# A top-k attention and MLP kernel: dividing the exponentials on GpSimd before their split, instead of the outputs after it

## The chip, the cores and the metric

The kernel runs on one core of a Trainium2 chip. The metric is the time of one execution in device microseconds (us), as the median of several runs. The engines are named as in the profile: PE is TensorE (matmuls; PEld its weight loads), DVE is VectorE, ACT is ScalarE, POOL is GpSimd, and SP is the engine whose queue issues nearly all DMAs. Each engine works through its instructions strictly in the order in which the program gives them; semaphores tie the engines to one another.

## The reference

Two stages follow each other. The first is attention in which each query keeps its 32 largest scores:

```python
B, H, S, D = 8, 8, 576, 64
scores = (1 / np.sqrt(D)) * np.matmul(q, k.transpose(0, 1, 3, 2))
kth = np.partition(scores, -32, axis=-1)[..., -32:-31]
scores = np.where(scores >= kth, scores, -1000000000.0)
scores = scores - np.max(scores, axis=-1, keepdims=True)
attn = np.exp(scores)
attn = attn / (np.sum(attn, axis=-1, keepdims=True) + 1e-09)
attn_out = np.matmul(attn, v)
```

The second takes the 4608 tokens (batch times sequence, 512 wide) through `h = x @ w_in` (512 x 2048), `g = h / (1 + exp(-1.702 h))` and `g @ w_out` (2048 x 512). All data is float32.

## The kernel before, in words

**Slots.** The attention is cut into 144 slots, 18 for each of the 8 batches. A slot is 128 query rows of two heads (or, for the last 64 rows of the sequence, 64 rows of four heads). A slot's scores are two blocks of 128 x 576. It goes through these steps:

- `scores` (L282): PE multiplies q and k into two PSUM tiles (`s_ps`; the pool has two buffers, so one slot's scores fill it). `copy_scores` (L294): ACT brings them to SBUF as `sc` (four buffers).
- `topk_of_pairs`: DVE finds the 32nd largest score of every row, a slot at a time. The two halves of a row are compared element by element (`pair_up`, L323: the larger ones go to `greater`; POOL makes the smaller ones, `lesser`, in two integer instructions, L326 and L327). Then come rounds of "the eight largest" (L344) and "take them out" (L347) over the larger ones, `pair_up` for the next slot, and two rounds over the smaller ones; a merge (L351) and a minimum (L356) give `cut`. These are 23 calls, counted from 0; `pair_up` of the next slot is call 14, the two last L344 are calls 19 and 20.
- `lows` (L377): POOL works out the bias `low` of the exponentials.
- `exponentials`: ACT masks the scores in place (L397, two instructions) and takes the exponentials (L400, two instructions, whose sums over the rows go to `sums`).
- `split` (L470): ACT copies the exponentials, taken as 16-bit words, into two planes of upper and lower halves, which are written over `sc`; SP writes them to DRAM (`rows`, L472). `turn_by_dma` (L478): a transposing DMA reads them back as `pt`, keys on the partitions.
- `values_at` (L538): PE multiplies v and `pt` into `o`.
- Division: the exponentials are not divided. `invert` (L429, L431) has DVE invert the sums of two slots at once, POOL spreads each over 64 columns (`wide`, L433), and PE transposes them (`sum_rows`, L527) into the same PSUM tile as `o`. ACT copies the tile to SBUF (L954, 128 x 512) and POOL multiplies `o` by the inverses into `xT` (`x_of`, L552).

**The MLP beside it.** When all 512 columns of 128 tokens stand in `xT`, they are a block. `hidden` (L595) multiplies four tiles' worth with `w_in` on PE, `tanh` (L617, L620) takes the tanh and a copy on ACT, `gate` (L629, L630) joins them on POOL, and `project` (L650) multiplies with `w_out`; a finished block leaves through ACT (L658) and SP.

**The order.** It is written out by hand. Slots 0 to 12 are handled singly by `slot`, while the weights are loaded, by a form of the steps that turns the exponentials on PE; there `divide` (L408, L410, L413) makes diagonal matrices of the inverses. From slot 13 on, `two_slots(n)` handles two slots in each call, n = 13, 15, ... I call one call an iteration. It takes the first of its slots through mask, exponentials and split, searches slot n, gives PE one `hidden` and one `project`, multiplies the values of slots n-3 and n-2, makes the scores of slots n+2 and n+3, takes slot n through mask, exponentials and split, gives PE another `hidden` and `project`, and searches slot n+1. Since every engine keeps the program's order, the order of these calls is the order on ACT, DVE, POOL and SP.

**q and k.** The q and k of a later batch are made ready one pair of heads at a time: `prepare_by_dma` copies their halves apart on ACT (L240, 24 times), and SP writes and transposes them (L244 to L249, L253). Batch 1 is turned on PE and copied by ACT instead (`prepare`, L217 to L224). All these calls fall on odd slots, into `prepare_some(first)` of an iteration.

In every search the inversion is one call among the 23:

```python
if i == (13 if m < SETTLED + 4 else 8) and m % 2:
    invert(m - 2)
```

Of the kernel before, what the change touches and what calls it, by code (L numbers as in the profile page):

```python
# [30 lines left out]
def kernel(  # L31
# [286 lines left out]
    def pair_up(n):  # L318

        sc = st[n]["sc"]  # L320
        a, b = sc[:, :, 0:HALF], sc[:, :, HALF:S]
        greater[n] = lefts.tile([P, 2, HALF], F32, name="greater", tag="left")
        nc.vector.tensor_tensor(out=greater[n][:], in0=a, in1=b, op=ALU.max)  # L323
        lesser[n] = raws.tile([P, 2, HALF], F32, name="lesser", tag="raw")
        whole = lesser[n][:].bitcast(I32)
        nc.gpsimd.tensor_tensor(out=whole, in0=a.bitcast(I32), in1=greater[n][:].bitcast(I32), op=ALU.subtract)  # L326
        nc.gpsimd.tensor_tensor(out=whole, in0=whole, in1=b.bitcast(I32), op=ALU.add)  # L327

    def topk_of_pairs(n):

# [59 lines left out]

    def exponentials(n, between=lambda: None):

        sc, cut, low = st[n]["sc"], st[n]["cut"], st[n]["low"]
        pr = st[n]["pr"] = prp.tile([P, 2 * S], F32, name="pr")
        den = st[n]["den"] = sums_of(n) if n >= SETTLED else small.tile([P, 2], F32, name="den")[:]
        for i in range(2):
            nc.scalar.activation(sc[:, i, :], sc[:, i, :], AF.Prelu, bias=cut[:, i : i + 1], alpha=HUGE)  # L397
        between()
        for i in range(2):
            nc.scalar.activation(  # L400
                pr[:, i * S : (i + 1) * S], sc[:, i, :], AF.Exp, bias=low[:, i : i + 1],
                accum_out=den[:, i : i + 1],
            )

    def divide(n):

        some = small.tile([P, 2], F32, name="some", tag="sums")
        nc.vector.tensor_scalar_add(some[:], st[n]["den"], 1e-9)  # L408
        rden = small.tile([P, 2], F32, name="rden", tag="inverse")
        nc.vector.reciprocal(rden[:], some[:])  # L410
        by = st[n]["by"] = xs[:, 4, 0:2, :]
        for i in range(2):
            nc.gpsimd.tensor_scalar(by[:, i, :], ident[:], rden[:, i : i + 1], 1.0, op0=ALU.mult, op1=ALU.mult)  # L413

    sums = {}

    def sums_of(n):

        k = n // 2
        if k not in sums:  # L420
            sums[k] = small.tile([P, 2, 2], F32, name="sums")
        return sums[k][:, n % 2, :]

    def invert(n):

        k = n // 2
        if k in sums:
            total = sums[k][:]
            nc.vector.tensor_scalar_add(total, total, 1e-9)  # L429
            inverse = small.tile([P, 4], F32, name="inverse")  # L430
            nc.vector.reciprocal(inverse[:], total.rearrange("p s j -> p (s j)"))  # L431
            wide = sums[k] = raws.tile([P, 2, 2, D], F32, name="wide", tag="raw")
            nc.gpsimd.tensor_copy(  # L433
                out=wide[:].rearrange("p s j d -> p (s j) d"),
                in_=inverse[:].unsqueeze(2).to_broadcast([P, 4, D]),
            )

    def turn(n, first, blocks):
# [41 lines left out]
    places = {}  # L480
    free = [4, 0, 1, 2, 3]

    def x_at(b, t, hp):

        name = (b, t) if t < NF else b // 2
        if name not in places:
            at = free.pop(1 if name in ((0, 0), (0, 1), (0, 2), (0, 3)) else 0)
            places[name] = at
        x = xs[:, places[name], hp, :]
        return x if t < NF else x[:, b % 2 * TAIL : (b % 2 + 1) * TAIL]  # L490

    def values(n, put_off=None):
# [29 lines left out]
            put_off.append(bring)  # L522


    def sum_rows(m, to):

        nc.tensor.transpose(to, sums[m // 2][:, m % 2, :, :], ident[:])  # L527

    def values_at(m, o):

        b, t, hps = slots[m]
# [12 lines left out]
                    )  # L544
        st[m].clear()

    def x_of(m, o, by):

        b, t, hps = slots[m]
        for p in range(2 if t == NF else 1):  # L550
            cols = slice(p * TAIL, (p + 1) * TAIL) if t == NF else slice(0, P)
            nc.gpsimd.tensor_tensor(out=x_at(b, t, hps[p]), in0=o[:, cols], in1=by[:, cols], op=ALU.mult)  # L552
        finish_x(m)

    def finish_x(m):

# [115 lines left out]
    def leave_all():  # L672
        while leaving:
            leaving.pop(0)()
# [40 lines left out]
    def finish_one():  # L715
        unfinished.pop(0)()
# [74 lines left out]
    def slot(n):  # L791
# [7 lines left out]
        if n == 0:  # L799
            for piece in some:  # L800
                piece["low"]()
                piece["sign"]()
        else:
            bounds(n - 1)
            if n == PAIRED:
                pair_up(n)

            exponentials(n - 1, bring_all if n % 4 == 1 else lambda: None)
            copy_scores(n + 1)
            bring_all()  # L810
            while signs:
                signs.pop(0)()
            if 1 < n <= TURNS:
                turn_main(n - 2)
                turn_ends(n - 2)
            for piece in some:
                piece["size"]()
            tanh(False)
        for i, op in enumerate(topk_of_pairs(n) if n >= PAIRED else topk(n)):
            op()  # L820
            if i == 2 and n < SETTLED:
                for _ in range(min(3 if n >= TURNS else 6, len(unfinished))):
                    finish_one()
            if i == 5:
                if n > 0:
                    divide(n - 1)
                while unfinished:
                    finish_one()
            if i == 10:
                gate(False)  # L830
# [47 lines left out]
    def two_slots(n):  # L878

        first, second = [later.pop(m, []) for m in (n, n + 1)]  # L880
        live = lambda m: 0 <= m < N
        aside = n < N

        def begin(todo):
            for fn, args in todo:
                if fn is not prepare and fn is not prepare_by_dma:
                    fn(*args)

        def prepare_some(todo):
            for fn, args in todo:  # L890
                if fn is prepare or fn is prepare_by_dma:
                    fn(*args)

        def find(m):
            for i, op in enumerate(topk_of_pairs(m) if live(m) else [lambda: None] * 23):
                op()
                if i == (13 if m < SETTLED + 4 else 8) and m % 2:
                    invert(m - 2)
                if i > 1 and unfinished:
                    finish_one()  # L900

        def project_one():
            if may_project(0):
                project(True)

        def measure(m):
            if live(m):
                bounds(m)
            gate(aside)

        opens = n == SETTLED + 1
        ahead = n < SETTLED + 4
        begin(first)
        measure(n - 1)
        if ahead:
            scores(n + 2)
        if opens:
            bring_all()
        if live(n - 1):
            exponentials(n - 1)  # L920
            split(n - 1)
        if ahead:
            copy_scores(n + 2)
        if opens:
            leave_all()
            tanh(aside)
        find(n)
        hidden(ps_t if opens else None)
        project_one()
        tanh(aside)  # L930
        prepare_some(first)
        held = [m for m in (n - 3, n - 2) if live(m) and "rows" in st[m]]
        o = ps_t.tile([P, 2, 2, P], F32, name="o", tag="tp") if held else None
        for i, m in enumerate(held):
            sum_rows(m, o[:, i, 0, :])
        if live(n + 2) and not ahead:
            scores(n + 2)
            copy_scores(n + 2)
        leave_all()
        for i, m in enumerate(held):  # L940
            values_at(m, o[:, i, 1, :])
        if live(n - 1):
            turn_by_dma(n - 1)
        while turns:
            turns.pop(0)()
        if live(n + 3):
            scores(n + 3)
        begin(second)
        measure(n)
        def bring():  # L950
            if not held:
                return
            x = raws.tile([P, 2, 2, P], F32, name="x", tag="raw")
            nc.scalar.copy(out=x[:], in_=o[:])  # L954
            for i, m in enumerate(held):
                x_of(m, x[:, i, 1, :], x[:, i, 0, :])

        if live(n):
            exponentials(n, bring)
        else:  # L960
            bring()
        if live(n):
            split(n)
            turn_by_dma(n)
        hidden(ps_t)
        if live(n + 3):
            copy_scores(n + 3)
        tanh(aside)
        prepare_some(second)
        project_one()  # L970
        leave_all()
        find(n + 1)

    with tc.manual_schedule():
        opening()
# [36 lines left out]
```

## Time and profile before

| what | us |
|---|---|
| median of three runs (1468.69 to 1471.01) | 1469.49 |
| the profiled execution's own time | 1468.81 |
| its span in the trace | 1467.0 |
| busy: PE / DVE / ACT / POOL | 1430.7 / 1336.3 / 1173.9 / 863.1 |
| L527 on PE, busy, 132 instructions | 25.3 |
| L552 and L433 on POOL, busy | 60.1 and 27.2 |
| L470 on ACT, 132 instructions, mean of one | 2.112 |

Busy times of an engine count overlapping instructions once. Matmuls are pipelined: a record of one lasts longer than the step from its start to the start of the next, so steps are read from starts. In rows of groups the columns are the line, the engine, the operation, what it writes and reads, and its count, then busy us and the mean ns of one, then the idle time before. In rows of the timeline they are the start and the length in us, the engine, the line and the operation. In rows of waits they are who waited for whom, us in total, how often, and the longest.

### The profile page before, as it was taken

How to read it: one execution, taken by the hardware profiler on the slowest of the kernel's cores; microseconds unless marked ns; L12 is line 12 of the kernel's file. 1: busy time of each engine (PE TensorE's matmuls, PEld its weight loads, DVE VectorE, ACT ScalarE, POOL GpSimd, SP SyncE). 2: the span in 40 equal slices, each digit the busy share in tenths (PEclk: the TensorE clock that was granted, in tenths of full speed). 3: DMA queues.
4: the chain of work that ended last, by engine and by line, in shares of the span. 5: the costliest groups of instructions: out<-in, count | busy, mean ns of one | idle time of the engine just before them, and what ended most of it. 6: DMA issues, size and time to landing. Idle time of an engine off the chain costs nothing.

```text
span 1467.0 us, 29219 instructions
## 1 busy us (share of the span) xinstructions
PE 1430.7 (98%) x9696; PEld 1015.8 (69%) x9696; DVE 1336.3 (91%) x4541; ACT 1173.9 (80%) x1865; POOL 863.1 (59%) x1119
## 2 busy tenths in 40 slices
PE   7789989999999999999999999999999999999998
PEld 5667757777666667777666667777666667777665
DVE  7999999999999999999999999999999999999910
ACT  6998788978788887878888787888878787887730
POOL 3777655666566665666665666656665666655510
PEclk8899999999999999999999999999999999999999
DMA  7452356867677677676777676766766777544420
GB/s 218 142 159 73 86 155 187 209 173 193 175 177 190 171 179 200 179 188 176 170 176 200 181 189 177 195 179 171 178 186 185 189 171 187 153 135 124 131 78 15
DMA packets 516311, 242.04 MB, mean 165 GB/s; under 512 B 452672, under 2 KB 490560, under 8 KB 516160
## 3 DMA queue, kind: packets, MB, share of 16 engines
q1 hardware_dynamic: 515728, 239.89, 62.2%
q8 instruction: 76, 1.25, 0.4%
q14 instruction: 75, 0.61, 0.1%
q10 hardware_dynamic: 432, 0.30, 0.1%
HBM read 45.09 MB, written 102.24 MB: 100 GB/s over the span
## 4 chain that ended last, share of the span: by engine, by line
PE 82%; DVE 13%; ACT 2%; issue 1%; DMA 1%; SPq 1%; POOL 0%; POOLq 0%; DVEq 0%; ACTq 0%
PE ph L595 31%; PE po L650 30%; PE o L538 10%; PE s_ps L282 10%; DVE top L304 4%; DVE left L307 3%; DVE top L344 2%; DVE left L347 1%; PE o L527 1%; DMA rows<-sc 1%; DVE greater L323 0%; DMA pt<-rows 0%; DVE lesser L347 0%; DVE th L632 0%; ACT pr L400 0%
## 5 line engine op out<-in xcount | busy, mean ns | idle before, releaser
L595 PEld LDWEIGHTS ph<-xT,win 128*128 128x128 f32 x3520 | 484.1, 191 | 86.9 <-issue 57.4
L595 PE MATMUL ph<-xT,win 128*128 128x128 f32 (+1 forms) x3520 | 537.6, 309 | 1.4 <-POOL xT L552 1.2
L650 PE MATMUL po<-wout,th 128*128 128x512 f32 x1152 | 518.4, 593 | 1.1 <-ACT ob L658 1.1
L650 PEld LDWEIGHTS po<-wout,th 128*128 128x128 f32 x1152 | 213.2, 190 | 214.5 <-issue 207.1
L344 DVE MAX8 top<-left 128x8 f32<-128x288 f32 x792 | 325.4, 445 | 0.0
L470 ACT COPY sc<-pr 128x2304 uint16<-128x2304 uint16 x132 | 278.8, 2112 | 4.2
L294 ACT ACTIVATE sc<-s_ps 128x576 f32<-128x576 f32 x288 | 171.0, 646 | 136.2 <-PE s_ps L282 133.9
L347 DVE MATCH_REPLACE8 left<-top,left 128x288 f32<-128x288 f32 x528 | 229.7, 442 | 0.0
L326 POOL TENSOR_TENSOR lesser<-sc,greater 128x576 int32<-128x576 int32 x132 | 186.6, 1413 | 72.8 <-DVE greater L323 72.8
L552 POOL TENSOR_TENSOR xT<-x 128x128 f32<-128x128 f32 (+1 forms) x148 | 60.1, 429 | 285.6 <-ACT x L954 285.6
L400 ACT ACTIVATE pr<-sc,low 128x576 f32<-128x576 f32 x288 | 221.3, 777 | 0.0
L397 ACT ACTIVATE sc<-sc,cut 128x576 f32<-128x576 f32 x288 | 208.1, 779 | 8.5 <-POOL cut L388 5.9
L344 DVE MAX8 top<-lesser 128x8 f32<-128x288 f32 x528 | 213.8, 445 | 0.0
L327 POOL TENSOR_TENSOR lesser<-lesser,sc 128x576 int32<-128x576 int32 x132 | 186.5, 1413 | 10.4
L282 PE MATMUL s_ps<-qk_t 64*128 64x288 f32 (+1 forms) x1280 | 182.2, 431 | 0.2 <-ACT qk_t L218 0.2
L630 POOL TENSOR_TENSOR th<-th,h 128x512 f32<-128x512 f32 x128 | 163.3, 1275 | 10.7
L629 POOL TENSOR_SCALAR th<-th 128x512 f32<-128x512 f32 x128 | 79.4, 620 | 110.3 <-ACT th L617 110.1
L538 PE MATMUL o<-pt,v_l 128*64 128x128 f32 (+1 forms) x2368 | 143.5, 264 | 0.1
L323 DVE TENSOR_TENSOR greater<-sc 128x576 f32<-128x576 f32 x132 | 101.8, 771 | 41.0 <-ACT sc L294 40.4
L538 PEld LDWEIGHTS o<-pt,v_l 128*64 128x64 f32 x2368 | 119.7, 137 | 25.5 <-issue 23.5
L282 PEld LDWEIGHTS s_ps<-qk_t 64*128 64x128 f32 (+1 forms) x1280 | 99.1, 177 | 41.1 <-issue 22.3
L617 ACT ACTIVATE th<-ph 128x512 f32<-128x512 f32 x144 | 85.9, 597 | 43.8 <-PE ph L595 40.8
(83 smaller groups left out, 1462.8 us busy)
## 6 DMA issues: line engine op xcount, KB each, us to landing
rows<-sc SPq DMA_DIRECT2D x132, 576.0 KB, 3.1
qk_rows<-halves SPq DMA_DIRECT2D x48, 256.0 KB, 2.8
qk_l<-in_q_dram SPq DMA_DIRECT2D x64, 128.0 KB, 3.0
raw<-in_moe_w_in_dram SPq DMA_DIRECT2D x16, 512.0 KB, 4.7
v_l<-in_v_dram SPq DMA_DIRECT2D x32, 256.0 KB, 3.3
raw<-in_moe_w_out_dram SPq DMA_DIRECT2D x16, 512.0 KB, 3.6
out_dram<-ob SPq DMA_DIRECT2D x32, 256.0 KB, 2.9
qk_l<-in_k_dram SPq DMA_DIRECT2D x62, 128.0 KB, 2.8
```

The source lines that it names most:

```text
L282: nc.tensor.matmul(ps[i][rows, c, 0:HALF], lhsT=qT[b, hps[p]][on, cols], rhs=kT[b, hps[p]][on, FIRST[i] + c * HALF : FIRST[i] + (c + 1) * ...
L294: nc.scalar.mul(out=to, in_=ps[i][:, :, 0:HALF], mul=SCALE)
L326: nc.gpsimd.tensor_tensor(out=whole, in0=a.bitcast(I32), in1=greater[n][:].bitcast(I32), op=ALU.subtract)
L327: nc.gpsimd.tensor_tensor(out=whole, in0=whole, in1=b.bitcast(I32), op=ALU.add)
L344: nc.vector.max(found(r, i, True), src[:, i, :])
L347: nc.vector.match_replace(to[:, i, :], found(r, i), src[:, i, :], LOWEST)
L397: nc.scalar.activation(sc[:, i, :], sc[:, i, :], AF.Prelu, bias=cut[:, i : i + 1], alpha=HUGE)
L400: nc.scalar.activation(pr[:, i * S : (i + 1) * S], sc[:, i, :], AF.Exp, bias=low[:, i : i + 1], accum_out=den[:, i : i + 1],)
L470: nc.scalar.copy(out=halves, in_=pr[:].bitcast(U16).rearrange("p (k h) -> p h k", h=2))
L538: nc.tensor.matmul(o[j * D : (j + 1) * D, cols], lhsT=main[:, j, c, :] if c < NF else tail[:, j, :], rhs=pt[:, MAIN[j] + c if c < NF else ...
L595: nc.tensor.matmul(ph[:, i * many * P : (i + 1) * many * P], lhsT=win[:, c, f * P : (f + 1) * P], rhs=xs[:, first : first + step * (many - ...
L650: nc.tensor.matmul(x.po[:], lhsT=gT[:, i * P : (i + 1) * P], rhs=wout[:, f, :], start=(x.done == 0), stop=(x.done == FC - 1))
```

## The change

The exponentials of the slots from 12 on are divided by their sums before they are split. Per slot, DVE inverts the two sums (`invert`, now for one slot, two columns), and POOL multiplies the two blocks of 128 x 576 exponentials in place (`normalize`). `sum_rows`, the spreading over 64 columns and the multiplication behind the values go away; ACT copies `o` straight into `xT`, 256 columns for two slots.

The order changes with it. The inversion of slot n-1 stands in the search of slot n, behind call 20 for odd n and behind call 18 for even n. The split of slot n-1 moves from before the search of slot n to behind it, behind `normalize`; likewise for slot n and the search of n+1. The mask of an iteration's second slot moves ahead of the scores' copy, except where q and k are prepared in the iteration. POOL's second instruction of `pair_up` (L327) is put off behind `normalize` and `lows`. `hidden` and `project` of the first half stand ahead of the search in the program.

```diff
@@ pair_up @@
-        nc.gpsimd.tensor_tensor(out=whole, in0=whole, in1=b.bitcast(I32), op=ALU.add)
+        unpaired.append(n)
+    def pair_rest():
+        while unpaired:
+            n = unpaired.pop()
+            whole, b = lesser[n][:].bitcast(I32), st[n]["sc"][:, :, HALF:S]
+            nc.gpsimd.tensor_tensor(out=whole, in0=whole, in1=b.bitcast(I32), op=ALU.add)
...
+    def invert(n):
+        some = small.tile([P, 2], F32, name="some", tag="sums")
+        nc.vector.tensor_scalar_add(some[:], st[n]["den"][:], 1e-9)
+        rden = st[n]["rden"] = small.tile([P, 2], F32, name="rden", tag="inverse")
+        nc.vector.reciprocal(rden[:], some[:])
...
+    def normalize(n):
+        pr = st[n]["pr"][:].rearrange("p (i k) -> p i k", i=2)
+        for i in range(2):
+            nc.gpsimd.tensor_scalar(
+                pr[:, i, :], pr[:, i, :], st[n]["rden"][:, i : i + 1], 1.0, op0=ALU.mult, op1=ALU.mult
             )
...
-    def sum_rows(m, to):
-        nc.tensor.transpose(to, sums[m // 2][:, m % 2, :, :], ident[:])
...
+    def x_of(held, o):
+        b, t, hps = slots[held[0]]
+        x = xs[:, place_of(b, t), :, :]
+        if t < NF:
+            nc.scalar.copy(out=x[:, hps[0] : hps[0] + 2, :], in_=o[:])
+        else:
+            parts = o[:].rearrange("p s (h r) -> p (s h) r", h=2)
+            nc.scalar.copy(out=x[:, :, b % 2 * TAIL : (b % 2 + 1) * TAIL], in_=parts)
+        for m in held:
+            finish_x(m)
```

`two_slots` after the change, from the definition of `find` on (`opens` holds in the first call, `ahead` in the first two; `mask` and `exps` are the two halves of `exponentials`):

```python
def find(m):
    for i, op in enumerate(topk_of_pairs(m) if live(m) else [lambda: None] * 23):
        op()
        if i == (20 if m % 2 else 18) and live(m - 1):
            invert(m - 1)
...
def measure(m):
    if live(m):
        lows(m)
    pair_rest()
    gate(aside)
...
if live(n - 1):
    exponentials(n - 1)
...
hidden(ps_t if opens else None)
project_one()
find(n)
if live(n - 1):
    normalize(n - 1)
tanh(aside)
measure(n)
if live(n - 1):
    split(n - 1)
prepare_some(first)
late = any(fn is prepare or fn is prepare_by_dma for fn, args in first)
if live(n) and not late:
    mask(n)
held = [m for m in (n - 3, n - 2) if live(m) and "rows" in st[m]]
if live(n + 2) and not ahead:
    scores(n + 2)
    copy_scores(n + 2)
o = ps_t.tile([P, 2, P], F32, name="o", tag="tp") if held else None
for i, m in enumerate(held):
    values_at(m, o[:, i, :])
if live(n - 1):
    turn_by_dma(n - 1)
...
if live(n + 3):
    scores(n + 3)
begin(second)
if live(n) and late:
    mask(n)
if live(n):
    exps(n)
if held:
    x_of(held, o)
leave_all()
hidden(ps_t)
if live(n + 3):
    copy_scores(n + 3)
find(n + 1)
if live(n):
    normalize(n)
    split(n)
    turn_by_dma(n)
tanh(aside)
measure(n + 1)
prepare_some(second)
project_one()
leave_all()
```

More of the change, by code (lines that the diff above doesn't have):

```diff
@@ L326, in pair_up @@
         nc.gpsimd.tensor_tensor(out=whole, in0=a.bitcast(I32), in1=greater[n][:].bitcast(I32), op=ALU.subtract)
-        nc.gpsimd.tensor_tensor(out=whole, in0=whole, in1=b.bitcast(I32), op=ALU.add)
+        unpaired.append(n)
+    unpaired = []
+    def pair_rest():
[3 more added lines that the diff above has]
+            nc.gpsimd.tensor_tensor(out=whole, in0=whole, in1=b.bitcast(I32), op=ALU.add)
     def topk_of_pairs(n):
@@ L391, in exponentials, with mask, exps @@
     def exponentials(n, between=lambda: None):
-        sc, cut, low = st[n]["sc"], st[n]["cut"], st[n]["low"]
-        pr = st[n]["pr"] = prp.tile([P, 2 * S], F32, name="pr")
-        den = st[n]["den"] = sums_of(n) if n >= SETTLED else small.tile([P, 2], F32, name="den")[:]
+        mask(n)
+        between()
+        exps(n)
+    def mask(n):
+        sc, cut = st[n]["sc"], st[n]["cut"]
         for i in range(2):
             nc.scalar.activation(sc[:, i, :], sc[:, i, :], AF.Prelu, bias=cut[:, i : i + 1], alpha=HUGE)
-        between()
+    def exps(n):
+        sc, low = st[n]["sc"], st[n]["low"]
+        pr = st[n]["pr"] = prp.tile([P, 2 * S], F32, name="pr")
+        den = st[n]["den"] = small.tile([P, 2], F32, name="den")
         for i in range(2):
@@ L403, in exponentials @@
             )
+    def invert(n):
[3 more added lines that the diff above has]
+        nc.vector.reciprocal(rden[:], some[:])
     def divide(n):
[L407 to L410, printed above, removed]
+        invert(n)
         by = st[n]["by"] = xs[:, 4, 0:2, :]
         for i in range(2):
[L413 to L435, printed above, removed]
+            nc.gpsimd.tensor_scalar(by[:, i, :], ident[:], st[n]["rden"][:, i : i + 1], 1.0, op0=ALU.mult, op1=ALU.mult)
+    def normalize(n):
[3 more added lines that the diff above has]
+                pr[:, i, :], pr[:, i, :], st[n]["rden"][:, i : i + 1], 1.0, op0=ALU.mult, op1=ALU.mult
             )
@@ L481, with place_of, x_at @@
     free = [4, 0, 1, 2, 3]
-    def x_at(b, t, hp):
+    def place_of(b, t):
         name = (b, t) if t < NF else b // 2
         if name not in places:
-            at = free.pop(1 if name in ((0, 0), (0, 1), (0, 2), (0, 3)) else 0)
-            places[name] = at
-        x = xs[:, places[name], hp, :]
+            places[name] = free.pop(1 if name in ((0, 0), (0, 1), (0, 2), (0, 3)) else 0)
+        return places[name]
+    def x_at(b, t, hp):
+        x = xs[:, place_of(b, t), hp, :]
         return x if t < NF else x[:, b % 2 * TAIL : (b % 2 + 1) * TAIL]
@@ L545, in values_at @@
         st[m].clear()
[L547 to L553, printed above, removed]
+    def x_of(held, o):
[8 more added lines that the diff above has]
+            finish_x(m)
     def finish_x(m):
@@ L818, in slot @@
             tanh(False)
+        pair_rest()
         for i, op in enumerate(topk_of_pairs(n) if n >= PAIRED else topk(n)):
             op()
+            pair_rest()
             if i == 2 and n < SETTLED:
@@ L892, in prepare_some @@
                     fn(*args)
+        opens = n == SETTLED + 1
+        ahead = n < SETTLED + 4
         def find(m):
@@ L896, in find, with measure @@
                 op()
-                if i == (13 if m < SETTLED + 4 else 8) and m % 2:
-                    invert(m - 2)
+                if i == (20 if m % 2 else 18) and live(m - 1):
+                    invert(m - 1)
                 if i > 1 and unfinished:
                     finish_one()
+        def measure(m):
+            if live(m):
+                lows(m)
+            pair_rest()
+            gate(aside)
         def project_one():
@@ L904, in project_one @@
                 project(True)
-        def measure(m):
-            if live(m):
-                bounds(m)
+        begin(first)
+        if opens:
+            bounds(n - 1)
             gate(aside)
[L911 to L914, printed above, removed]
         if ahead:
@@ L920, in two_slots @@
             exponentials(n - 1)
-            split(n - 1)
         if ahead:
@@ L926, in two_slots @@
             tanh(aside)
-        find(n)
         hidden(ps_t if opens else None)
         project_one()
+        find(n)
+        if live(n - 1):
+            normalize(n - 1)
         tanh(aside)
+        measure(n)
+        if live(n - 1):
+            split(n - 1)
         prepare_some(first)
+        late = any(fn is prepare or fn is prepare_by_dma for fn, args in first)
+        if live(n) and not late:
+            mask(n)
         held = [m for m in (n - 3, n - 2) if live(m) and "rows" in st[m]]
-        o = ps_t.tile([P, 2, 2, P], F32, name="o", tag="tp") if held else None
-        for i, m in enumerate(held):
-            sum_rows(m, o[:, i, 0, :])
         if live(n + 2) and not ahead:
@@ L938, in two_slots @@
             copy_scores(n + 2)
-        leave_all()
+        o = ps_t.tile([P, 2, P], F32, name="o", tag="tp") if held else None
         for i, m in enumerate(held):
-            values_at(m, o[:, i, 1, :])
+            values_at(m, o[:, i, :])
         if live(n - 1):
@@ L948, in two_slots @@
         begin(second)
[L949 to L956, printed above, removed]
-        if live(n):
[L959 to L964, printed above, removed]
+        if live(n) and late:
+            mask(n)
+        if live(n):
+            exps(n)
+        if held:
+            x_of(held, o)
+        leave_all()
         hidden(ps_t)
@@ L967, in two_slots @@
             copy_scores(n + 3)
+        find(n + 1)
+        if live(n):
+            normalize(n)
+            split(n)
+            turn_by_dma(n)
         tanh(aside)
+        measure(n + 1)
         prepare_some(second)
@@ L971, in two_slots @@
         leave_all()
-        find(n + 1)
     with tc.manual_schedule():
```

## The prediction

> **What bounds the kernel now.** I read the busy row of the page first, then the stretches of 100 us, the waits by engine, and last the order in time of two iterations from 700 to 740 us.
>
> ```profile
> PE 1430.7 (98%) x9696; PEld 1015.8 (69%) x9696; DVE 1336.3 (91%) x4541; ACT 1173.9 (80%) x1865; POOL 863.1 (59%) x1119
> ```
> ```profile
> 700.00:800.00 100.00, 100.00 (x561) 68.57 (x558) 95.50 (x342) 83.85 (x129) 62.18 (x83) 1.00 0.74 183
> ```
> ```profile
> DVE greater L323 <- ACT sc L294: 40.4, 53, 1.0
> ```
> In steady state (columns of the second row: width, then busy us of PE, PEld, DVE, ACT, POOL, then the clock) PE is never idle at full clock, but DVE works 95.5 of 100 us and has one regular wait, for the scores' copy. Two engines are nearly full; what counts is how little DVE has to spare. The starts of L323 for the even slots run from 144.95 (slot 12) to 1372.27 (slot 142): 65 iterations in 1227.3 us, 18.88 each. The chain in order of time gives an iteration of PE:
>
> ```profile
> 715.24 0.22 PE o L527 x2
> 715.46 1.17 PE s_ps L282 x8
> 716.63 2.33 PE o L538 x40
> 718.96 1.17 PE s_ps L282 x8
> 720.13 3.65 PE ph L595 x16
> 723.78 3.43 PE po L650 x8
> 727.22 3.45 PE ph L595 x16
> 730.67 3.43 PE po L650 x8
> ```
> They add to 18.85. One slot's search on DVE takes 8.89 without a wait or an inversion (the commonest spacing of L323 before 385 us), so two with today's one inversion (0.28) are 18.06: DVE spares 0.8 us an iteration, most of it idle at L323 (0.57 and 0.67 in these two).
>
> **What goes and what comes.** PE loses L527: 0.22 x 66 = 14.5 us, all on the path. POOL loses L552 (60.1 us) and L433 (27.2), ACT about 0.2 us an iteration (a copy of 256 columns, not 512): none of it on the path, beyond the 1.2 and 2.9 us that PE and PEld waited for L552. DVE gets two inversions of two columns for one of four: +0.28 an iteration, so 18.34 at least; the reciprocal between the last search and the merge covers a 0.11 dependency, so 18.23. That would still lie under PE's new 18.63.
>
> POOL gets four multiplications of 128x576 an iteration. No row shows that size. L377, the same form over one column, takes 0.268; L413, over 128 columns, 0.375: 0.84 ns a column, so 0.75 for 576. L629, another form, 0.62 for 512, would scale to 0.70 as its low end; L326, with two inputs, is 1.41 at most. I take 0.75, the same form's slope, and 1.47 for a pair (L413's pairs take 0.72 to 0.74). POOL goes from 62 to about 71 of 100 us, not a bound by its load.
>
> **The new loop.** The time is set by where the division stands. The split on ACT now waits for POOL's multiplications, those for the inversion near the end of the search on DVE; behind the split ACT keeps, in order, the next slot's mask, the scores' copy, and the exponentials. DVE's next L323 waits for that copy, and its next inversion for those exponentials. That is a circle through DVE, POOL, ACT and DVE. Its ACT rows:
>
> ```profile
> 721.20 2.11 ACT L470 COPY sc<-pr 128x2304 uint16<-128x2304 uint16 x1
> 723.22 1.18 ACT L294 ACTIVATE sc<-s_ps 128x576 f32<-128x576 f32 x2
> 724.29 0.60 ACT L617 ACTIVATE th<-ph 128x512 f32<-128x512 f32 x1
> 724.77 0.60 ACT L620 COPY h<-ph 128x512 f32<-128x512 f32 x1
> 725.24 1.47 ACT L397 ACTIVATE sc<-sc,cut 128x576 f32<-128x576 f32 x2
> 726.58 0.79 ACT L400 ACTIVATE pr<-sc,low 128x576 f32<-128x576 f32 x1
> ```
> Starts show what each holds ACT for: split 2.02, copy 1.07 (its end, 1.18 or 1.19), mask 1.34; the exponentials take 1.63 (719.54 to 721.17). From the start of the first slot's split:
> - split 2.02, mask 1.34, copy and hop to DVE 1.29 (716.66 to L323 at 717.95): L323 at 4.65;
> - L323 to the end of that search 3.46 (708.39 to 711.85), inversion 0.28 and 0.06 of blocking (below): 8.45;
> - the next search up to its inversion, which stands behind the last L344: 5.44 to L323 (721.41 to 727.13 less the 0.28) and 2.99 (717.95 to 720.21, and 0.73): 16.88;
> - inversion until written 0.36 (706.00 to 706.36), hop to POOL 0.10 (waits of this kind end 0.06 to 0.17 after), two multiplications 1.47, hop to ACT 0.04: 18.85, where the next such split starts.
>
> DVE's own work in it is 18.23; the rest is its wait at L323 (0.56) and the blocking. So an ordinary iteration becomes 18.85 again: PE's gain is lost to the loop.
>
> **The q/k iterations.** All 24 copies of L240 (2.02 us of ACT) fall into the first slot of an iteration, behind the split, four in every nine iterations. There the mask goes behind the scores' copy:
>
> ```profile
> 695.70 2.12 ACT L240 COPY halves<-qk_l 128x2304 uint16<-128x2304 uint16 x1
> 697.72 1.21 ACT L294 ACTIVATE sc<-s_ps 128x576 f32<-128x576 f32 x2
> ```
> L323 comes at 2.02 + 2.02 + 1.29 = 5.33, 0.68 later. The exponentials end at 4.04 + 1.07 + 1.34 + 1.63 + 0.03 = 8.11; DVE stands at its inversion at 5.33 + 2.25 = 7.58 (708.39 to 710.64) and waits 0.53, which takes in the 0.06. Together 1.15: 20.00 us. Behind this waiting inversion stand the rest of the search and so every later one. PE, at 18.63, cannot win it back: its next score products wait for a free bank, that is for the same copy. In today's order L240 delays nobody, for ACT waits 3.7 us for PE in such a half.
>
> **Sum.** 24 iterations at 20.00; the four that prepare batch 1 have smaller copies (L218, 0.59 each, for L240), at an estimated 19.3; 37 at 18.85: 480.0 + 77.2 + 697.5 = 1254.7, against 1227.3: +27.4. The tail keeps its order and loses three L527 pairs and the wait for L552 (1.08 at 1384.43): about -1.5. The profiled execution took 1468.81 (span 1467.0), so 1494.7; the median of the runs lies 0.7 above it: **1495 us**.
>
> **Edits at nothing, and their cover.** The move of L327 behind the multiplications: it ends 2.0 us after the split starts, and its reader comes 3.4 us later; beyond that it costs one for one. The second half's circle (inversion, multiplications, split, tanh and h, mask, exponentials) brings the exponentials 1.6 us before their inversion. The rows transfer of a first slot starts some 9 us later and must land before the copy of the second scores of the iteration reuses its buffer: 3.1 us to land, 5.5 at most, against about 4.4 of ACT work between; that copy has 1.3 more before the next split, so 0 to 1 us in rare iterations. SP holds each transposition 2.5 us and is passed by four or five transfers in a half; pt lands (4.8, at most 7.4) 2 to 9 us ahead of its matmuls. In 29 iterations the second hidden product reads an x copied behind the exponentials: PE waits 0.4, or 1.7 with q/k, which is inside what it idles there.
>
> **A rule weighed.** DVE's L429 took 0.15 alone and this beside a POOL multiply:
>
> ```profile
> 252.03 1.30 POOL L630 TENSOR_TENSOR th<-th,h 128x512 f32<-128x512 f32 x1
> ```
> ```profile
> 252.11 1.25 DVE L429 TENSOR_SCALAR sums<-sums 128x4 f32<-128x4 f32 x1
> ```
> It ended with POOL's instruction. In the new order both inversions and both L323 meet an idle POOL, but for 0.06: L326 ends 2.31 after L323 starts, the inversion comes at 2.25. The Trainium skill, "SBUF — State Buffer", in its passage on the shared port pair, says that a VectorE instruction with two SBUF inputs, as L323 is, or in a two-port mode, is shut out for the whole of a GpSimd instruction. Taken without the order, with POOL busy 71% and half an instruction to wait (0.6), four such starts would be an estimated 1.7 us an iteration, 112 us in all; by the order it is the 0.06 of the sum.
>
> **Rivals.**
> - *PE stays the bound* (1454: 1468.8 - 14.5 and a little of the waits). The place is the loop; it decides once an ordinary iteration is under 18.63 and a q/k iteration too. PE's full rows speak for it; against it, 1.4 us would have to be missing from rows that agree within 0.1. Chance 0.10.
> - *The change hides L240 only* (the q/k iterations cost what others do): 65 x 18.85 = 1225, so about 1466. Chance 0.06, half on either side of the bound.
> - *The loop is shorter*: multiplications at 0.66 each (the slope of L413 to L629) and the shortest hops, 0.27 less: about 1480, the low end of the forecast; between 1470 and that, chance 0.08.
> - *L323 is shut out by the gate's multiply* in each ordinary iteration: POOL is through 0.8 us before L323; if that cover goes, up to 1.28 x 37 = 47 us: 1542. Chance 0.08.
> - *Forecast*, 1480 to 1515: 0.68. The upper end adds 0.3 an iteration for longer hops and the reused buffer.
>
> The range 1468 to 1520 leaves out the first rival, part of the second and most of the fourth. A measurement of this kernel tells about 0.2% (3 us) from no change: faster 0.13, same 0.06, slower 0.81.
>
> **What would show it.** PE idle before L282, for ACT's copy; DVE waiting about 0.5 us at L323 in ordinary iterations, and 1.2 there plus 0.5 at the inversion where L240 runs; ACT idle some 2.5 us ahead of each first split, released by POOL; iterations of 18.85 and 20.0; multiplications of 0.75. Wrong would be: PE still at 100 of 100 us with iterations of 18.63 (first rival), or L323 or the inversion starting at the end of a POOL instruction (fourth).

## The result, and the profile after

The changed kernel takes 1505.39 us (median of four runs, 1503.56 to 1507.8) against 1470.25 before: a ratio of 1.0241, with a 95% interval of 1.0222 to 1.026. It is slower by 35 us; the forecast was 1495, slower by 25.5. The profiled execution took 1506.29, with a span of 1504.5.

The busy row of its page:

```profile
PE 1440.3 (96%) x9564; PEld 1011.5 (67%) x9564; DVE 1343.4 (89%) x4672; ACT 1159.3 (77%) x1865; POOL 971.2 (65%) x1171
```

and the same 100 us as before (width, then PE, PEld, DVE, ACT and POOL, then the clock):

```profile
700.00:800.00 100.00, 96.92 (x621) 66.67 (x622) 93.45 (x338) 79.03 (x121) 67.69 (x83) 1.00 0.66 173
```

PE, which was full, now idles 3 of 100 us, and DVE is less busy too. No engine is full: the time is in a loop between them. Its waits, from the list by engine (who waited for whom, us in total, times, longest):

```profile
ACT sc L477 <- POOL pr L441: 130.2, 117, 4.9
POOL pr L441 <- DVE top L360: 90.8, 66, 3.0
DVE greater L323 <- ACT sc L294: 53.8, 63, 2.6
POOL pr L441 <- DVE rden L428: 37.8, 43, 3.2
DVE some L426 <- ACT pr L418: 24.9, 38, 6.3
ACT sc L294 <- DMA rows<-sc: 23.0, 15, 3.6
```

The split (now L477) waits for POOL's multiplications (L441), those for DVE's inversion (L426, L428), L323 for the scores' copy, the inversion for the exponentials (L418): the circle of the prediction, link by link. The last of these waits stands in the q/k iterations, the first few and at the end (the 6.3); from slot 24 on, an ordinary iteration's inversion does not wait. One round of it, in an ordinary iteration, on DVE and POOL:

```profile
405.48 0.16 DVE L426 TENSOR_SCALAR some<-den 128x2 f32<-128x2 f32 x1
405.67 0.17 DVE L428 RECIPROCAL rden<-some 128x2 f32<-128x2 f32 x1
...
412.14 0.76 DVE L323 TENSOR_TENSOR greater<-sc 128x576 f32<-128x576 f32 x1 [0.52 <-ACT sc L294]
```
```profile
406.00 1.47 POOL L441 TENSOR_SCALAR pr<-pr,rden 128x576 f32<-128x576 f32 x2 [1.26 <-DVE top L360]
```

and on ACT:

```profile
407.51 2.11 ACT L477 COPY sc<-pr 128x2304 uint16<-128x2304 uint16 x1 [0.34 <-POOL pr L441]
409.53 1.44 ACT L410 ACTIVATE sc<-sc,cut 128x576 f32<-128x576 f32 x2
410.87 1.17 ACT L294 ACTIVATE sc<-s_ps 128x576 f32<-128x576 f32 x2
```

The inversion starts at 405.48, the pair of multiplications takes 1.47 from 406.00, the split starts at 407.51, and L323 follows 4.63 later, having waited 0.52. From 402.52 to 421.32, the L323 of two even slots, this iteration takes 18.80 (predicted 18.85). PE's own work would have allowed 18.63.

Ahead of these multiplications the rows name L360, the merge, as it is the DVE instruction that ended last (405.95). The inverses were written at 405.84, 0.16 before the multiplications start; in the second half of the iteration, where the rows name L428, it is the same 0.16 (414.76 to 414.92).

### The profile page after: what moved, and what is told of

Same layout as the page of the kernel before. It is cut to its first block, busy times and chain, and to the rows that moved or that the text cites. A ratio compares the mean times of both kernels' runs of the same rounds, so it can differ in the third digit from the quotient of the medians.

```text
span 1504.5 us, 29163 instructions
## 1 busy us (share of the span) xinstructions
PE 1440.3 (96%) x9564; PEld 1011.5 (67%) x9564; DVE 1343.4 (89%) x4672; ACT 1159.3 (77%) x1865; POOL 971.2 (65%) x1171
## 5 line engine op out<-in xcount | busy, mean ns | idle before, releaser
L605 PE MATMUL ph<-xT,win 128*128 128x128 f32 (+1 forms) x3520 | 541.3, 310 | 19.1 <-ACT xT L558 12.1
L605 PEld LDWEIGHTS ph<-xT,win 128*128 128x128 f32 x3520 | 484.6, 191 | 108.0 <-issue 53.8
L477 ACT COPY sc<-pr 128x2304 uint16<-128x2304 uint16 x132 | 278.8, 2112 | 130.5 <-POOL pr L441 130.2
L353 DVE MAX8 top<-left 128x8 f32<-128x288 f32 x792 | 320.8, 446 | 0.0
L441 POOL TENSOR_SCALAR pr<-pr,rden 128x576 f32<-128x576 f32 x264 | 194.1, 748 | 144.3 <-DVE top L360 90.8
L418 ACT ACTIVATE pr<-sc,low 128x576 f32<-128x576 f32 x288 | 219.5, 766 | 0.0
L282 PE MATMUL s_ps<-qk_t 64*128 64x288 f32 (+1 forms) x1280 | 199.8, 437 | 2.7 <-ACT sc L294 2.2
L282 PEld LDWEIGHTS s_ps<-qk_t 64*128 64x128 f32 (+1 forms) x1280 | 110.9, 180 | 85.7 <-issue 50.9
L323 DVE TENSOR_TENSOR greater<-sc 128x576 f32<-128x576 f32 x132 | 102.8, 779 | 53.8 <-ACT sc L294 53.8
```

The costliest lines, as they stand in the source:

```text
L282: nc.tensor.matmul(ps[i][rows, c, 0:HALF], lhsT=qT[b, hps[p]][on, cols], rhs=kT[b, hps[p]][on, FIRST[i] + c * HALF : FIRST[i] + (c + 1) * ...
L353: nc.vector.max(found(r, i, True), src[:, i, :])
L418: nc.scalar.activation(pr[:, i * S : (i + 1) * S], sc[:, i, :], AF.Exp, bias=low[:, i : i + 1], accum_out=den[:, i : i + 1],)
L441: nc.gpsimd.tensor_scalar(pr[:, i, :], pr[:, i, :], st[n]["rden"][:, i : i + 1], 1.0, op0=ALU.mult, op1=ALU.mult)
L477: nc.scalar.copy(out=halves, in_=pr[:].bitcast(U16).rearrange("p (k h) -> p h k", h=2))
L605: nc.tensor.matmul(ph[:, i * many * P : (i + 1) * many * P], lhsT=win[:, c, f * P : (f + 1) * P], rhs=xs[:, first : first + step * (many - ...
```

## Experiments

Twelve kernels: some price one side of the change by itself, some add to the circle or open it, and some vary the order. All times are medians; ratios are to the kernel before, with their 95% intervals.

**old_no_divisors: the gain by itself.** It leaves out the division: L527 goes, POOL multiplies by columns of the weights.

```diff
-        for i, m in enumerate(held):
-            sum_rows(m, o[:, i, 0, :])
...
-            nc.scalar.copy(out=x[:], in_=o[:])
+            nc.scalar.copy(out=x[:, :, 1, :], in_=o[:, :, 1, :])
...
-                x_of(m, x[:, i, 1, :], x[:, i, 0, :])
+                x_of(m, x[:, i, 1, :], wout[:, 0, 0:P])
```

> The kernel before without its 132 L527: the inverses are not turned, ACT copies only the values' half of the tile, and POOL multiplies with columns of the weights in their place, so the output is not divided by the sums. It prices the gain by itself. Theory: 0.22 us in each iteration in which PE is the bound, which is from 385 us on, 53 of them: 11.7 us, 1458. Rival (DVE is the bound already): 1469.

Measured: 1453.4, ratio 0.989 (0.9875 to 0.9905). So 16.5 us were to be had, the whole of L527's 14.5 and a little more: from slot 22 to slot 142 the L323 of even slots span 1122.1 us, against 1136.0 before; the head and the tail gave the rest. The expectation of 11.7 was too small: the iterations up to slot 36, though DVE-bound, passed on 3.4 us as well.

**old_loaded: POOL's load by itself.** The kernel before, with two idle multiplications behind each gate; the result is the same.

```diff
             gate(aside)
+            if aside:
+                idle = raws.tile([P, 2, S // 2], F32, name="idle", tag="raw")
+                for i in range(2):
+                    nc.gpsimd.tensor_scalar(
+                        idle[:].rearrange("p i k -> p (i k)"), win[:, i, 0:S],
+                        ident[:, 0:1], 1.0, op0=ALU.mult, op1=ALU.mult
+                    )
```

> The kernel before, with two idle multiplications of 128x576 on POOL behind each gate, which nobody waits for: POOL's added load, 198 us, without the circle. Theory: POOL goes from 62 to about 78 of 100 us and DVE's inversion and L323 may meet one of them now and then, in the 0.6 us an iteration that DVE idles: 1470 to 1480. Rival (load): 1500.

Measured: 1471.15, ratio 1.0002 (0.9992 to 1.0011): nothing, with POOL at 78 of 100 us:

```profile
700.00:900.00 200.00, 200.00 (x1250) 137.25 (x1251) 194.20 (x677) 166.94 (x256) 156.58 (x205) 1.00 0.72 181
```

PE stays at 200 of 200. POOL even shut L323 out 60 times, 23.1 us in all, inside the time that DVE idles anyway. In this place the load costs nothing.

**no_multiply: the circle opened.** The changed kernel without its two calls of `normalize`; the output is not divided.

> The changed kernel without POOL's multiplications (264 of 128x576); the sums are still inverted, so the output is not divided by them. The split no longer waits for POOL, so the circle is open; every other step and its order stay. Theory: PE becomes the bound, as in old_no_divisors (1453), with some of the first iterations' loss left: 1455 to 1462. Rival (the order itself, the later splits and their transfers, costs the time whatever POOL does): 1475 or more.

Measured: 1467.3, ratio 0.998 (0.9971 to 0.999), 38 us less than with the multiplications. It lies between the two expectations: 14 us more than old_no_divisors remain. They stand in the q/k iterations: from slot 32 on, those with L240 take 19.1 to 19.8 us each, against 18.2 to 19.1 of the others. Behind L240 the exponentials still come 0.43 late for the inversion, and L323 often 0.2 to 0.9. The first iterations are back at what they were before (91.4 us from slot 12 to 22; 91.3 before, 97.9 after the change). So the 52 us between PE's gain alone and the changed kernel are 38 for the multiplications in the circle and 14 for the order around them, which stay when nothing is multiplied.

**twice_first and twice_second: which multiplications count.** The first, or the second, slot of each iteration is multiplied a second time by 1.0; the result is the same.

```diff
-    def normalize(n):
+    def normalize(n, times=1):
...
-        for i in range(2):
+        for i in range(2 * times):
+            by = st[n]["rden"][:, i : i + 1] if i < 2 else 1.0
...
-            normalize(n - 1)
+            normalize(n - 1, 2)
```

> The first slot's exponentials are multiplied on POOL a second time, by 1.0; the result is the same. Theory: those two multiplications (1.47 us a pair) lie on the circle, so each of 65 iterations grows by 1.47: 1505 + 95 = 1600. Rival (POOL is a cost by its load): POOL goes from 68 to 76 of 100 us, which is still no bound, so at most 20 us.

> The changed kernel with the second slot's exponentials multiplied a second time by 1.0, as twice_first does with the first slot's. POOL has the same added load in both. Theory: the second slot's multiplications are not on the circle, with 1.6 us to spare up to the next inversion, so 1.47 more costs 0 to 0.3 us an iteration: 1505 to 1525. Rival (load): the same as twice_first, 1590.

Measured: twice_first 1590.1 (1.0822; 1.0806 to 1.0838), twice_second 1554.1 (1.0576; 1.0559 to 1.0592). The first is the theory's, with one size off: by an immediate a pair takes 1.31 and not 1.47 (the second line; the line numbers in these rows are those of the two kernels, which from L441 on differ by one from the changed kernel's):

```profile
1169.69 1.47 POOL L442 TENSOR_SCALAR pr<-pr,rden 128x576 f32<-128x576 f32 x2 [1.25 <-DVE top L360]
1171.12 1.31 POOL L442 TENSOR_SCALAR pr<-pr 128x576 f32<-128x576 f32 x2
```

and ordinary iterations grow by 1.27, from 18.79 to 20.06. The second is a miss: 48.7 us where I expected at most 20, though less than the load rival's 84.7. Ordinary iterations grow by 0.95, and not by way of the exponentials and the inversion. On ACT, on POOL and then on DVE:

```profile
643.58 2.11 ACT L476 COPY sc<-pr 128x2304 uint16<-128x2304 uint16 x1 [2.01 <-POOL pr L442]
645.60 0.59 ACT L626 ACTIVATE th<-ph 128x512 f32<-128x512 f32 x1
```
```profile
646.28 0.62 POOL L638 TENSOR_SCALAR th<-th 128x512 f32<-128x512 f32 x1 [0.88 <-ACT th L626]
646.99 1.27 POOL L639 TENSOR_TENSOR th<-th,h 128x512 f32<-128x512 f32 x1
```
```profile
647.19 1.69 DVE L323 TENSOR_TENSOR greater<-sc 128x576 f32<-128x576 f32 x1
```

The added pair moves the second slot's split back, with it the tanh that stands behind it on ACT, and with that the gate's multiply on POOL, until the next L323 starts beside it. L323 then takes 1.69 in place of 0.74: it is through 0.62 after the multiply ends. With the long L323 at about 152 us, which stands beside another POOL instruction (L144) in every kernel here, there are 62 of them, 58.1 us over the usual 0.76 in all. This is the prediction's fourth rival, brought about by 1.31 us of POOL. It also gives that rival's cover in the changed kernel: 1.31 - 0.95 = 0.36, not the 0.8 that I had given it. The changed kernel's own trace comes near that: the multiply ends some 0.2 ahead of an even slot's L323 (below, at 421.10 for the L323 at 421.32), and an L323 that starts beside it is still 0.62 from its end when the multiply is through, which hides another 0.12 of its 0.74. Only ahead of an odd slot's L323 are there 0.85.

```profile
419.83 1.27 POOL L640 TENSOR_TENSOR th<-th,h 128x512 f32<-128x512 f32 x1
```

The gate takes the tanh of the same half, which ACT makes behind the split (`th L626` in the row); I had it take the older one.

**halves_late and mask_first: two ways to shorten the circle.** The first moves L240 behind the iteration's last scores' copy and so lets the mask stand early everywhere but for batch 1; the second moves the second slot's mask ahead of the split.

```diff
-        prepare_some(first)
-        late = any(fn is prepare or fn is prepare_by_dma for fn, args in first)
+        prepare_some([x for x in first if x[0] is prepare])
+        late = any(fn is prepare for fn, args in first)
...
             copy_scores(n + 3)
+        prepare_some([x for x in first if x[0] is prepare_by_dma])
```
```diff
         measure(n)
+        if live(n):
+            mask(n)
         if live(n - 1):
             split(n - 1)
         prepare_some(first)
-        late = any(fn is prepare or fn is prepare_by_dma for fn, args in first)
-        if live(n) and not late:
-            mask(n)
...
-        if live(n) and late:
-            mask(n)
```

> The 24 copies of L240 move from behind the first split to behind the copy of the iteration's last scores; the mask then stands ahead of the scores' copy in those iterations too. Theory (the circle of inversion, multiplications, split, mask, copy and L323 sets the time, and L240 lengthens it): those 24 iterations fall from 20.0 to 20.7 us to the ordinary 18.8, 37 us in all, so about 1469. Rival (POOL's added load and its port are the cost, wherever ACT's copies stand): no more than 5 us, about 1501.

> In every iteration the second slot's mask stands ahead of the first slot's split, in the time in which ACT waits for POOL; nothing else moves. Theory: the circle loses the mask's 1.34 us, so ordinary iterations fall to the 18.63 of PE (7 us in 37), and q/k iterations to about 19.6 to 19.9, since their L323 still waits for split, L240 and copy (12 us in 24): about 1487. Rival (POOL's load and port): nothing, 1505.

Measured: halves_late 1478.7 (1.006; 1.0045 to 1.0075), mask_first 1485.3 (1.0108; 1.0091 to 1.0125). Both go the theory's way and against the rival's: POOL's work is the same in both, and 27 and 20 us go by moving ACT instructions. mask_first comes within 2 us of what was expected, in part because two misses offset each other: from slot 22 on its ordinary iterations average 18.53 (most 18.2 to 19.0), a little under the 18.63 expected, and its q/k iterations 20.04 (19.6 to 20.6), a little over the 19.6 to 19.9. halves_late falls 10 us short. Its q/k iterations average 19.10, not 18.8, and something new is late: ACT waits 62.1 us in 23 places (23.0 in 15 before the move) for the rows transfer of a slot whose score buffer is written again, and that pushes the gate into L323 eleven times (5.3 us).

**both: the two together.**

> Mask ahead of the split in every iteration, and L240 behind the last scores' copy. Theory: the circle is at 17.6 us everywhere, PE at 18.63 becomes the bound in 61 iterations, the four that prepare batch 1 stay near 20: about 49 us less than the changed kernel, 1457, so faster than before by about 0.9%. Rival (POOL's load and port): 1500.

Measured: 1471.8, ratio 1.0012 (1.0003 to 1.0021), over ten runs. It missed by 15 us. The circle is gone, and the next things in line take its place:

```profile
ACT sc L294 <- DMA rows<-sc: 96.2, 29, 6.1
DVE some L426 <- ACT pr L418: 31.0, 28, 6.1
```

The wait for the score buffer has grown to 96.2 us, and PE waits for a late `pt` now and then (2.20 us at 895.78). Where neither happens, from 1257 us on, iterations are PE's: 18.87 against 19.09 before, the 0.22 of L527.

**both_five, five_early, five_later, gate_older: the next limits.** both_five gives the scores a fifth buffer (and `raws` six for seven, for the room). five_early also moves batch 1's turns ahead of the first split, five_later does so from the second iteration on, gate_older is five_later with the gate ahead of the tanh of its half, in both halves. The edits of both_five, of five_early against both_five, and of gate_older against five_later:

```diff
-    raws = pool("raws", 7)
+    raws = pool("raws", 6)
...
-    scp = pool("scp", 4)
+    scp = pool("scp", 5)
```
```diff
             normalize(n - 1)
+        prepare_some([x for x in first if x[0] is prepare])
         tanh(aside)
...
             split(n - 1)
-        prepare_some([x for x in first if x[0] is prepare])
```
```diff
+        measure(n)
         tanh(aside)
-        measure(n)
...
+        measure(n + 1)
         tanh(aside)
-        measure(n + 1)
```

> The kernel `both` with five score buffers in place of four (and six of the pool `raws` in place of seven, for the room). In `both`, ACT waits 96.2 us in 29 places for the rows transfer of a slot whose score buffer is to be written again, ahead of the split of the next slot. Theory (with the circle shortened, that transfer is what is late next): the waits go, and with them most of DVE's waits at the inversion (31 us): about 10 us less, 1462. Rival (DVE and POOL shut each other out, whatever ACT does): no change, 1472.

> As both_five, and the q and k of batch 1 are turned on PE and copied by ACT ahead of the first split, in the time in which ACT waits for POOL. Theory: the four first iterations, 79.7 us in `both` against 73.1 before, lose most of that: 6 us less than both_five, about 1456. Rival (they are slow by PE's lower clock, 0.94 from 190 to 300 us, and not by the wait for ACT): no change.

> As five_early, but in the first iteration (slot 13) the q and k of batch 1 stay behind the split, since there the early place made DVE wait 5.3 us at one inversion (iteration of 23.5 us). Theory: that wait goes, and the rest is PE-bound at what the kernel without divisors shows (18.70 an iteration from slot 22 on, against 18.85 in five_early): 1467.6 - 5 = 1462 to 1463, faster than before by 0.5%. Rival (POOL's load and port leave no gain, as wherever time is won DVE and POOL give it back): 1467 to 1470.

> As five_later, with the gate ahead of the tanh of the same half, so that POOL joins the half before's tanh, which is ready, and is through earlier ahead of L323. In five_early POOL's L640 shuts L323 out 25 times, 16.3 us in all. Theory of the port: those long L323 (1.2 to 1.8 us) all but vanish, to under 5; as PE is the bound there, the time falls by 0 to 4 us, 1459 to 1463. Rival (the long L323 come from something else than the multiply ahead of them): as many long L323 as before.

| kernel | us (median) | ratio, 95% interval | slots 12 to 22 | slots 22 to 142 |
|---|---|---|---|---|
| before | 1470.25 | | 91.3 | 1136.0 |
| changed | 1505.4 | 1.0241 (1.0222 to 1.026) | 97.9 | 1167.7 |
| both | 1471.8 | 1.0012 (1.0003 to 1.0021) | 97.4 | 1136.3 |
| both_five | 1470.25 | 1.000 (0.9991 to 1.0009) | 96.5 | 1133.3 |
| five_early | 1467.6 | 0.9984 (0.9975 to 0.9994) | 97.9 | 1131.2 |
| five_later | 1471.3 | 1.0012 (1.0002 to 1.0022) | 95.6 | 1132.9 |
| gate_older | 1487.2 | 1.011 (1.0095 to 1.0124) | 96.7 | 1150.5 |
| old_no_divisors | 1453.4 | 0.989 (0.9875 to 0.9905) | 90.6 | 1122.1 |

(The last two columns are from the starts of L323 in the profiled executions, which differ from the medians by up to 3 us; five_later's, at 1468.4, is its fastest.) The wait for the rows transfer is gone in both_five, as expected, but it bought 1.5 us and not 10. five_early fell by 3, not 6: the first iterations only moved their loss into the one that starts with slot 14's L323 (23.5 us), where an inversion waits 5.3 us for its exponentials; ahead of those, ACT waits 6.4 us for the first of the early turns. five_later came to 1471.3 and not 1462: there the next iteration (22.5 us) has such a wait, of 4.2. Both show that one iteration's early turn is another's late exponential. gate_older bears out the port and nothing else: the long L323 fall from 25 to 1, yet the time grows by 16 us, with L323 waiting 49.2 us for the scores' copy (14.1 in five_later) and PE 18.6 us for `pt` in 21 places. Why the moved gate brings those on isn't settled. The best version that divides on POOL is five_early, 0.16% under the kernel before (0.06 to 0.25%).

## Why the prediction was right, and by how much it was short

- **The mechanism held.** The circle of inversion, multiplications, split, mask, copy and L323 takes PE's place as the bound. Ordinary iterations: 18.85 forecast, 18.78 to 18.80 measured in most, with L323 waiting 0.52 (forecast 0.56). POOL's multiplication: 0.75 forecast by the slope of the same form, 0.747 measured; by the slope to L629 (0.66) it would have been wrong. That the circle is the cause is shown from four sides: adding to it (twice_first), opening it (no_multiply), shortening it on ACT alone (mask_first, halves_late), and adding the same load elsewhere (old_loaded).
- **The q/k iterations held too.** 20.00 forecast; nine of the twelve first ones of a pair take 19.99 to 20.01, with L323 waiting 1.20 and the inversion 0.43 (forecast 1.24 and 0.53).
- **PE stays the bound**, the first rival, fell: 1453 is there without the division (old_no_divisors), not with it in this place. The second, that the q/k iterations cost what others do, fell as well: all 24 take 20.0 us or more, against 18.8. The third, a shorter loop by cheaper multiplications, fell with the 0.747. The fourth happened, but in few iterations (below).
- **Two signs did not show as written.** PE was to idle before L282, for ACT's copy, and does so for 2.2 us in the whole run; it idles before L605 instead, mostly for `xT` (L558), a wait that the prediction had put inside PE's idle time:

```profile
L605 PE MATMUL ph<-xT,win 128*128 128x128 f32 (+1 forms) x3520 | 541.3, 310 | 19.1 <-ACT xT L558 12.1
L282 PE MATMUL s_ps<-qk_t 64*128 64x288 f32 (+1 forms) x1280 | 199.8, 437 | 2.7 <-ACT sc L294 2.2
```

  ACT was to idle 2.5 us ahead of each first split, released by POOL. In the round above it idles 2.53 for the tanh's input from PE (at 406.10) and then 0.34 for POOL; outside the first iterations the wait for POOL there is 1.9 at most. POOL still comes last, so the sum's step, from the multiplications to the split, stands.
- **The tail** gave the 1.5 us forecast (94.7 us from the L323 of slot 142 to the end before, 93.3 after).
- **What was mis-sized** is the sum of the iterations: 1254.7 forecast, 1265.6 measured (slot 12 to slot 142, 145.66 to 1411.25), 10.9 short. Three terms make it up:
  - *The second q/k iteration of a pair*: 20.2 or 20.73, not 20.0; with the three long L323 below, the 24 add up to 488.2, not 480.0. A finished block's copy (L668) is queued on ACT ahead of the mask. I had given it its 0.48 of work, but PE, delayed by the first of the pair, makes ACT wait for it: 1.48 in the one and 2.01 in the other kind, and the inversion is late by what the slack does not cover (0.64 in the latter).

```profile
362.94 0.60 ACT L668 ACTIVATE ob<-po 128x512 f32<-128x512 f32 x1 [2.01 <-PE po L660]
363.43 1.43 ACT L410 ACTIVATE sc<-sc,cut 128x576 f32<-128x576 f32 x2
```

  - *The iterations that prepare batch 1*: 80.2 for the four, not 77.2, and 20.8 in the next, not 18.85. I took the copies' size (L218) and left out that PE sits between two of them: its next transposition (L221) waits for a PSUM tile that ACT frees behind the split.

```profile
229.77 0.48 PE L221 MATMUL tp<-ident,qk_l 128*128 128x128 f32 x1 [6.84 <-ACT qk_t L218]
230.26 2.69 PE L282 MATMUL s_ps<-qk_t 64*128 64x288 f32 x8
```

  - *The cover of L323 against POOL*: 0.36 and not 0.8. It holds nearly always (five long L323 in the whole run, 3.9 us, the one beside L144 among them), but the buffer wait that I had put at 0 to 1 us "in rare iterations" is 23.0 us in 15, up to 3.6, and where it delays the tanh, the gate runs into L323: at 614.45 that takes 1.69.
- Ordinary iterations gave 2 us back. Together: 8.2 + 3.0 + 2.0 - 2.2 = 11.0, the 10.9 but for rounding; the third term is part of the 8.2.
- **The rule that was weighed** (the Trainium skill, "SBUF — State Buffer", on the shared port pair) holds in the traces read here: L323, with two SBUF inputs, started beside a GpSimd instruction, ends only after that is through (0.62 after it in the rows of twice_second). As the prediction had it, the order decides and not the odds (an estimated 112 us by those): 3.9 us in the changed kernel and 58.1 in twice_second, whose POOL is only 9% busier. Its price also depends on who waits: 23.1 us of it in old_loaded cost nothing.

## What to carry to other kernels

Moving work from a full engine to an idle one did not pay here, because the receiving instruction lies on a circle of in-order engines that became the bound: write such a circle out from row durations and see which step is queued behind the new wait, since four multiplications an iteration that were free as load behind the gate (old_loaded) cost 38 us as a link. When an ACT instruction waits, everything behind it in the program waits too, so put what is ready (the mask, the q/k copies) ahead of the wait; then expect the next late thing, here a transfer and a buffer, to be a fraction of a us behind. Price a copy that another engine must feed by that engine's state in that iteration, not by its length.

## What the runs showed of the hardware

PE ran slowly after a pause. After the 6.84 us wait above, eight L282 took 2.69 us, against 1.24 where PE had not paused, and the granted clock (the last columns are clock, DMA share and GB/s) was 0.52 from 229 to 236 us, where the same stretch of the kernel before is at 1.00:

```profile
222.00:229.00 7.00, 0.94 (x9) 0.70 (x7) 6.93 (x27) 2.10 (x3) 4.71 (x6) 0.75 0.67 146
229.00:236.00 7.00, 6.22 (x41) 5.02 (x43) 4.36 (x15) 5.07 (x13) 1.28 (x1) 0.52 0.51 152
```

After a wait of 5.09, at 208.43, eight L282 took 2.29. So these long waits of PE cost more than their length. On POOL, the same `tensor_scalar` over 128x576 took 0.747 with its factor from SBUF, and by an immediate a pair took 1.31 in place of 1.47.
